# Gated mix of local and full attention on one core: the last rows of the first two tiles computed behind all others, first weights in larger pieces, and copies of the last units on VectorE

## The chip, the core and the metric

The kernel runs on one core of one Trainium2 chip. A core has five engines, each with an instruction queue of its own that is worked off in order: TensorE (PE: matrix products; PEld is its loading of weights), VectorE (DVE), ScalarE (ACT), GpSimd (POOL) and SyncE (SP, which here only issues transfers). They meet at semaphores. Transfers between main memory and the on-chip memory run on 16 DMA engines; in this kernel they are issued by SP, and a few of the first ones by ACT, and each of the two issuers has a queue of its own. Matrix products land in PSUM, eight banks of 128 rows by 512 numbers.

The metric is the time of one execution in microseconds (us) on the device. Before the change it was 901.09 us, the median of three runs from 900.93 to 901.24.

## The reference

Two attentions over the same 2048 rows of 448 numbers, 16 heads of 28 each, are mixed by a gate computed from the input. The setup draws all inputs in float32.

```python
x = A_x
g = _sigmoid((x * gate_w).sum(-1, keepdims=True))
a = _A_ref(x, A_wqkv, A_wo)    # each row attends to 8 earlier rows, 2 apart
b = _B_ref(x, B_wqkv, B_wo)    # each row attends to all rows
return g * a + (1 - g) * b

# _B_ref
q, k, v = qkv[0], qkv[1], qkv[2]
scores = jnp.einsum("bhqd,bhkd->bhqk", q, k) * (Dh ** -0.5)
p = _softmax(scores, axis=-1)
o = jnp.einsum("bhqk,bhkd->bhqd", p, v)
return (lambda x, *d: x.transpose(*d))(o, 0, 2, 1, 3).reshape(B, S, D) @ wo
```

## The kernel before

**Two parts of each number.** The products want more precision than one pass of the matrix engine gives. So a value is split into a rounded part (`hi`, type fp32r) and the rest (`lo` = value minus `hi`), and a product is the sum of hi by hi, hi by lo and lo by hi. The rounding is a copy (on ACT, `split` at L223, or a cast on DVE), the rest is a subtraction (on DVE or POOL).

**First stage: the projections.** The 448 input rows (the transposed input has one row for each of its 448 features) make three blocks of 128 and a tail of 64. The tail's `hi` stands in one half of the 128 partitions and its `lo` in the other, and the tail of the weights is loaded twice (`both`, L228), so that one product of the tail does the work of two. A tile of the result is 128 columns of weights by 512 input columns (a quarter `nb` of the 2048 positions), and takes 11 products (`ORDER`, L294): a triple (a, c, k) says whether the `lo` of the input (a) or of the weights (c) is used, and which block of rows (k). The first ten tiles (`FULL`) sum all their products in one PSUM bank (`project`, L314); after that tiles are cut in halves that run side by side. The list `tiles` (L449) fixes the order of the tiles; the first three use the three blocks of columns of weight set 0: columns 448 to 576 (place `wa`, 128 to 256, in `wh0`/`wl0`), 0 to 128, and 576 to 704. Tile 0 has an order of its own, `FIRST` (L296), and three products on zeros (`warm(3)`) behind its first one. Before it nine such products run while nothing has been loaded (`warm(9)`, L215). When a tile is done, `qk_tile` (L352) copies it out, splits it and stores both parts to main memory.

**The first loads** (L403 to L418). In the order of the program: the weights of tile 0 (`wr0`, three blocks of 128 columns, SP), blocks 0 and 1 of the first quarter of the input (ACT's queue), its block 2 and its tail (SP), the weights' tails for two tiles, the weights of tile 1 and then of tile 2 (`wr1`, 128 columns each), the third tail, and then the other three quarters of the input. A transfer from the ninth on is issued when the eighth before it has landed, since eight semaphores are used in turn. From L419 follow the roundings and rests: ACT first makes four zero tiles (`QP`, L422) that are wanted much later, then rounds the weights of tile 0, input block 2, the tail and the other weights; DVE rounds input blocks 0 and 1 and makes the rests; POOL makes the rest of tile 0's weights (L429). The splitting of the second quarter of the input (`split_x(1)`) stands behind tile 0, that of the third tile's weights (`split_third`) ahead of it.

**Second stage: full attention.** 16 units of 16 steps. Unit u has four heads (u // 4) and a quarter of the queries (u % 4); step kt has 128 of the keys. A step (`scores`, L966) makes 12 products for the scores of four heads into four PSUM banks, two exponentials of 128x1024 on ACT (L994) and, one step later, four products with V into the bank pair of `av` (L952, L955; each is shown as two rows). As long as maxima of later units are still to be found, a step also has up to three products of a first pass (L144) and the maxima of them on DVE (L150). The last maxima are done in step 234 of 256; the 21 steps from there have none, and I call them the **bare steps**. At a unit's end `fin_copy` takes `av` out of PSUM (it stands one step into the next unit, before that step's exponentials on ACT, and the next product into `av` waits for it); the sums are inverted, spread, multiplied (`fin_on`, POOL), and `fin_hi` rounds the result, `fin_lo` makes its rest and `fin_store` stores both. For unit 13 `fin_hi` comes in step 237, for unit 14 in step 255, `fin_copy` of unit 14 in step 241. `load_q` (L117) loads the next unit's queries in step kt = 12, together with its maxima (`nm`), which stand in two extra rows of the same tile.

The local attention's vector work runs on POOL and DVE beside this. In the last two units DVE also splits the weights of the output projection (`split_wo`, L782).

**Third stage: the output projection**, 16 tiles of 21 products (`op_tile`, L933; products at L841), whose first nine products are put ahead of the last products with V.

## Time and profile before

| | |
|---|---|
| median of the runs shown | 901.09 us (900.93 to 901.24) |
| the profiled execution's own time | 900.67 us |
| its span, first to last instruction | 898.9 us |
| busy: PE, DVE, ACT, POOL | 892.2, 738.2, 644.5, 641.0 us |
| first product on PE (on zeros) begins | 1.45 us |
| first product on data begins | 5.74 us |
| scores of the first bare step begin (see the second stage) | 782.55 us |
| last product of the output projection ends | 895.25 us |

The profiled execution was 0.42 us shorter than the median of the runs. Between its own time and its span lie 1.8 us that no engine shows.

How to read the rows: a timeline row gives start and duration in us, the engine, the source line, the operation, what it writes and reads with shapes, how many instructions were merged into the row, and in brackets how long the engine had been idle before it and what it waited for. An engine named with a q (SPq, ACTq) is the engine's queue issuing a transfer. A row of windows gives for each engine the busy us and the number of instructions in a stretch, then the clock that PE was granted (1.00 is full), the mean busy share of the DMA engines, and what they moved in GB/s. Matrix products overlap, so that a row's duration is longer than the distance at which such products follow each other.

### The profile page before, as it was taken

To read this page: it belongs to the slowest core of one execution; us is meant where nothing else is said; L and a number is where in the kernel's file an instruction comes from. 1 tells how busy PE (TensorE), PEld (TensorE's weight loads), DVE (VectorE), ACT (ScalarE), POOL (GpSimd) and SP (SyncE) were. 2 spreads that over 40 slices of the span, in tenths; PEclk is the share of its full clock that TensorE was granted. 3 is DMA by queue.
4 is the path that set the end of the run, shared out by engine and by line. 5 is a ranking of instruction groups with operands and counts; after the bars stand their busy time and mean duration, and the time that the engine had idled before them with its cause. 6 is when DMAs were issued, how large, how long until landed. Compare 5 with 4: busy or idle time off the path is not lost.

```text
span 898.9 us, 20542 instructions
## 1 busy us (share of the span) xinstructions
PE 892.2 (99%) x8326; PEld 533.8 (59%) x8326; DVE 738.2 (82%) x961; ACT 644.5 (72%) x770; POOL 641.0 (71%) x507
## 2 busy tenths in 40 slices
PE   8999999999999999999999999999999999999998
PEld 6888999999954444444444444444444444434997
DVE  6588999999979999999999999999999999821220
ACT  7456434343378888898988989889888898898220
POOL 2489846464469689999999999999999699501000
PEclk9999999999999999999999999999999999999999
DMA  8887403459472241225224242342220322245791
GB/s 267 282 252 191 151 12 84 134 139 104 120 243 70 94 132 46 76 50 157 70 57 145 82 116 67 84 137 65 56 65 19 89 43 57 75 104 156 220 285 53
DMA packets 116470, 104.51 MB, mean 116 GB/s; under 512 B 77160, under 2 KB 84712, under 8 KB 115592
## 3 DMA queue, kind: packets, MB, share of 16 engines
q1 hardware_dynamic: 116088, 102.68, 41.6%
q8 instruction: 65, 1.06, 0.5%
q10 hardware_dynamic: 288, 0.52, 0.2%
q14 instruction: 29, 0.24, 0.1%
HBM read 62.20 MB, written 40.96 MB: 115 GB/s over the span
## 4 chain that ended last, share of the span: by engine, by line
PE 98%; ACT 1%; DMA 1%; SPq 0%; issue 0%; DVE 0%; ACTq 0%
PE T L989 31%; PE av L955 28%; PE r L312 15%; PE T L841 8%; PE r L307 8%; PE r L144 4%; PE T L144 4%; DMA raw<-in_wB 1%; ACT P L994 0%; SPq L230 0%; ACT raw L375 0%; PE av L1039 0%; SPq L240 0%; ACT wh L224 0%; ACT onhi L892 0%
## 5 line engine op out<-in xcount | busy, mean ns | idle before, releaser
L994 ACT ACTIVATE P<-T 128x1024 f32<-128x1024 f32 x512 | 496.7, 1024 | 59.9 <-PE T L989 57.6
L150 DVE TENSOR_REDUCE MX<-T 128x1 f32<-128x512 f32 x470 | 442.1, 954 | 33.9 <-PE T L144 19.1
L955 PE MATMUL av<-P,V 128*32 128x512 f32 x2048 | 272.7, 605 | 0.4 <-ACT osb L859 0.4
L989 PEld LDWEIGHTS T<-QH,KH 30*128 30x128 f32 x1024 | 92.6, 181 | 230.6 <-ACT P L994 197.3
L144 PE MATMUL T<-KH,QP 28*128 28x512 f32 x704 | 220.0, 455 | 0.1
L989 PE MATMUL T<-QH,KH 30*128 30x512 f32 x1024 | 212.6, 489 | 0.2 <-ACT P L994 0.2
L166 DVE TENSOR_REDUCE MX<-r 128x2 f32<-128x1024 f32 x160 | 192.5, 1221 | 22.8 <-PE r L144 20.2
L989 PE MATMUL T<-QH,KL 28*128 28x512 f32 x1024 | 187.0, 395 | 0.0
L989 PE MATMUL T<-QL,KH 28*128 28x512 f32 x1024 | 184.9, 392 | 0.0
L618 POOL TENSOR_TENSOR prod<-qt,kt 128x896 f32<-128x896 f32 x64 | 135.4, 2115 | 5.1 <-DMA kt<-a_scr 5.0
L375 ACT ACTIVATE raw<-r 128x896 f32<-128x896 f32 (+1 forms) x64 | 58.9, 921 | 96.8 <-PE r L312 94.5
L144 PE MATMUL r<-KH,QP 64*128 64x512 f32 x320 | 105.0, 392 | 0.0
L679 POOL TENSOR_TENSOR oat<-oat,prod 128x896 f32<-128x896 f32 x48 | 101.3, 2110 | 2.0
L144 PEld LDWEIGHTS T<-KH,QP 28*128 28x128 f32 x704 | 86.0, 181 | 27.4 <-ACT P L994 19.4
L376 POOL TENSOR_TENSOR ast<-raw 128x448 f32<-128x448 f32 x48 | 55.5, 1155 | 57.9 <-ACT raw L375 48.2
L674 POOL TENSOR_TENSOR prod<-vt,L 128x896 f32<-128x896 f32 x56 | 95.4, 1704 | 0.2
L989 PEld LDWEIGHTS T<-QL,KH 28*128 28x128 f32 x1024 | 94.2, 184 | 0.0
L989 PEld LDWEIGHTS T<-QH,KL 28*128 28x128 f32 x1024 | 93.5, 183 | 0.5
L312 PE MATMUL r<-wh,xh 64*128 64x448 f32 (+1 forms) x512 | 93.3, 363 | 0.0
L955 PEld LDWEIGHTS av<-P,V 128*32 128x32 f32 x2048 | 40.3, 108 | 77.8 <-issue 65.0
L312 PEld LDWEIGHTS r<-wh,xh 64*128 64x128 f32 x512 | 75.1, 185 | 0.4
L312 PE MATMUL r<-wh,xl 64*128 64x448 f32 (+1 forms) x384 | 73.4, 364 | 0.0
(112 smaller groups left out, 1120.7 us busy)
## 6 DMA issues: line engine op xcount, KB each, us to landing
a_scr<-ast SPq DMA_DIRECT2D x24, 448.0 KB
qk_hi<-qkh SPq DMA_DIRECT2D x24, 256.0 KB
qk_lo<-qkh SPq DMA_DIRECT2D x24, 256.0 KB
rbc<-rs SPq DMA_DIRECT2D x64, 64.0 KB
QP<-qk_hi SPq DMA_DIRECT2D x64, 56.0 KB
KL<-qk_lo SPq DMA_DIRECT2D x16, 224.0 KB
QH<-qk_hi SPq DMA_DIRECT2D x64, 56.0 KB
QL<-qk_lo SPq DMA_DIRECT2D x64, 56.0 KB
```

Source lines behind the costliest of these rows:

```text
L144: nc.tensor.matmul(bank, qhis[u][h % 2][r, 128 * qs:128 * qs + 128], KH[u // NB % 3][r, 512 * kc:512 * kc + 512], start=True, stop=True)
L150: i = nc.vector.tensor_reduce(MX[:, n % NMX:n % NMX + k], bank, axis=X, op=ALU.max)
L166: nc.vector.tensor_reduce(m, PM[k], axis=X, op=ALU.max)
L307: nc.tensor.matmul(bank, ws[c][rows, k, t[4]:t[4] + 128], x, start=first, stop=last)
L312: nc.tensor.matmul(bank[:, 0:cols], x, ws[c][rows, k, 0:cols], start=first, stop=last)
L618: nc.gpsimd.tensor_tensor(out=p, in0=qt[c], in1=kvt["k", c % 2][:, HALO - DIL * w:HALO - DIL * w + NJ, :], op=ALU.mult)
L674: nc.gpsimd.tensor_tensor(out=dst.rearrange("p j (h d) -> p j h d", d=DH), in0=kvt["v", c % 2][:, HALO - DIL * w:HALO - DIL * w + NJ, :].r ...
L679: nc.gpsimd.tensor_tensor(out=ows[c % 2][:, :, 0:56] if w == W - 1 else oat[c], in0=oat[c], in1=oat[c, w], op=ALU.add)
L841: writes(bank, nc.tensor.matmul(bank[:, :D], src, wo[c][k], start=(first and k == ks[0] and i == 0), stop=(last and k == ks[-1] and i == 2)))
L955: nc.tensor.matmul(av[32 * h:32 * h + 32, :], V[:, kt, 4 * g + h, :], tiles_[h], start=(kt == 0), stop=(kt == NJ - 1), skip_group_check=True)
L989: nc.tensor.matmul(bank[a], (KH[g % 3], KH[g % 3], KL[g % 2])[t][r, ks], (qh, ql, qh)[t][r, :], start=(t == 0), stop=(t == 2))
L994: e = nc.scalar.activation(p, one if a == "2" else mine, AF.Exp, scale=SCALE).ins
```

## The change

Three groups of edits.

**The first loads.** The weights of tile 0 and of tile 2 (columns 448 to 704) are loaded in one transfer of 256 columns, the weights of tile 1 in a second one; all three blocks of the first quarter of the input go by ACT's queue; the weights' tails are loaded as 256 and 128 columns in place of 128, 128 and 128. Only two of the four zero tiles are made first.

**The first products.** Tiles 0 and 1 both get an order of their own, without the products of the tail rows (k = 3); these four follow behind both tiles. Tile 0 now has its first rest-of-input product in second place and mixes blocks as their parts are made; tile 1 does hi by hi, lo by hi, hi by lo. `warm(3)` is gone. ACT rounds input blocks 1 and 2 (before: 2 alone), DVE makes all rests of the weights, three blocks in one instruction (before: POOL for tile 0's, single blocks for the others). Both tiles are copied out behind tile 1, and the splitting of the second quarter stands behind them.

**The last units.** `fin_copy` of unit 14 and `fin_hi` of units 13 and 14 run on DVE; the queries of unit 15 are loaded three steps earlier than its maxima.

```diff
-    def load_q(u):
+    def load_q(u, low=True):
         Qs[u] = load_part(u, "QH", qk_hi), load_part(u, "QL", qk_lo)
+        if low:
+            load_nm(u)
+
+    def load_nm(u):
...
-        FIRST = [(0, 0, 0), (0, 1, 0), (0, 0, 1), (0, 1, 1), (0, 0, 2), (0, 1, 2),
-                 (1, 0, 0), (1, 0, 1), (1, 0, 2), (0, 0, 3), (0, 1, 3)]
+        FIRST = [[(0, 0, 0), (1, 0, 0), (0, 0, 1), (0, 1, 0), (0, 1, 1), (0, 0, 2), (0, 1, 2), (1, 0, 1), (1, 0, 2)],
+                 [(0, 0, 0), (0, 0, 1), (0, 0, 2), (1, 0, 0), (1, 0, 1), (1, 0, 2), (0, 1, 0), (0, 1, 1), (0, 1, 2)]]
...
         def project(n):
-            order = FIRST if n == 0 else ORDER
+            order = FIRST[n] if n < 2 else ORDER
             for i, p in enumerate(order):
-                product(n, p, None, i == 0, i == len(order) - 1)
-                if n == 0 and i == 0:
-                    warm(3)
+                product(n, p, None, i == 0, n > 1 and i == len(order) - 1)
+            if n == 1:
+                for m in range(2):
+                    product(m, (0, 0, 3), None, False, False)
+                    product(m, (0, 1, 3), None, False, True)
...
-        nc.sync.dma_start(wr0, wB[0:384, 448:576].rearrange("(k p) c -> p k c", p=128))
-        load_x(0, 0, 1, nc.scalar)
-        load_x(0, 1, 2, nc.scalar)
-        load_x(0, 2, 3)
+        nc.sync.dma_start(wr0[:, :, 0:256], wB[0:384, 448:704].rearrange("(k p) c -> p k c", p=128))
+        for kt in range(3):
+            load_x(0, kt, kt + 1, nc.scalar)
+        nc.sync.dma_start(wr1, wB[0:384, 0:128].rearrange("(k p) c -> p k c", p=128))
         load_tails(0, 1)
...
-        for t in (*QP[0], *QP[1]):
+        for t in QP[0]:
             nc.scalar.activation(t, t0, AF.Copy)
...
+        nc.vector.tensor_copy(xh[0][:, 0, :], r[:, 0, :])
+        low_x(0)
+        split(wh0[:, 0:3, wa], wl0[:, 0:3, wa], wr0[:, :, 0:128])
+        for kt in (1, 2):
+            nc.scalar.activation(xh[0][:, kt, :], r[:, kt, :], AF.Copy)
+            low_x(kt)
+        split(wh0[:, 0:3, wb], wl0[:, 0:3, wb], wr1)
+        nc.scalar.activation(tail[0:64], t[0:64], AF.Copy)
         nc.vector.tensor_tensor(out=tail[64:128], in0=t[0:64], in1=tail[0:64].bitcast(F32), op=ALU.subtract)
...
+        split(wh0[:, 3, 0:384], wl0[:, 3, 0:384], wt0[:, 0:384])
+        split(wh0[:, 0:3, wc], wl0[:, 0:3, wc], wr0[:, :, 128:256])
+        for t in QP[1]:
+            nc.scalar.activation(t, t0, AF.Copy)
...
-                qk_tile(n, t[2], t[3])
+                for m in {0: (), 1: (0, 1)}.get(n, (n,)):
+                    qk_tile(m, *tiles[m][2:4])
...
-            if n == 0:
+            if n == 1:
                 split_x(1)
...
-        nc.scalar.activation(t, av, AF.Copy)
+        if u == NU - 2:
+            nc.vector.tensor_copy(t, av)
+        else:
+            nc.scalar.activation(t, av, AF.Copy)
...
-        nc.scalar.activation(fin["hi"], fin["on"], AF.Copy)
+        if NU - 4 < u < NU - 1:
+            nc.vector.tensor_copy(fin["hi"], fin["on"])
+        else:
+            nc.scalar.activation(fin["hi"], fin["on"], AF.Copy)
...
-            if kt == 12 and u + 1 < NU:
+            if u + 2 < NU and kt == 12:
                 load_q(u + 1)
+            elif u + 2 == NU and kt == 9:
+                load_q(u + 1, False)
+            elif u + 2 == NU and kt == 12:
+                load_nm(u + 1)
```

How the instructions stand on the engines that the prediction speaks of. First, PE at the start of the program, before the change; `r_140` takes the products on zeros, `r_128` is the bank of tile 0 and `r_132` that of tile 1, `xh`/`xl` are the two parts of the input, `wh`/`wl` of the weights. Rows that read the same as one shown are left out here and below.

```order
L213 MATMUL r_140<-t_161 128x512 x9
L307 MATMUL r_128<-xh_180,wh_188 128x512
L213 MATMUL r_140<-t_161 128x512 x3
L307 MATMUL r_128<-xh_180,wl_189 128x512
L307 MATMUL r_128<-xh_180,wh_188 128x512
L307 MATMUL r_128<-xh_180,wl_189 128x512
L307 MATMUL r_128<-xh_180,wh_188 128x512
L307 MATMUL r_128<-xl_184,wh_188 128x512 x3
L307 MATMUL r_132<-xh_180,wh_188 128x512 x4
```

And the same place after it:

```order
L217 MATMUL r_140<-t_161 128x512 x9
L311 MATMUL r_128<-xh_180,wh_188 128x512
L311 MATMUL r_128<-xl_184,wh_188 128x512
L311 MATMUL r_128<-xl_184,wh_188 128x512 x2
L311 MATMUL r_132<-xh_180,wh_188 128x512 x3
L311 MATMUL r_132<-xl_184,wh_188 128x512 x3
L311 MATMUL r_132<-xh_180,wl_189 128x512 x3
L311 MATMUL r_128<-xh_180,wh_188 128x512
L311 MATMUL r_132<-xh_180,wl_189 128x512
L311 MATMUL r_136<-xh_180,wh_188 128x512 x4
```

Tile 0 now ends, but for its tail, with two products that need the rest of input blocks 1 and 2; tile 1's nine follow, then the four of the tails, and only then tile 2 (`r_136`).

Second, ACT at the start, after the change; `raw` is the wide piece of weights, `wr_192` the weights of tile 1, `wt_191` the tails.

```order
L423 ACTIVATE QP_155<-t_161 128x512
L423 ACTIVATE QP_156<-t_161 128x512
L228 ACTIVATE wh_188<-raw 128x3x128
L436 ACTIVATE xh_180<-V 128x512 x2
L228 ACTIVATE wh_188<-wr_192 128x3x128
L439 ACTIVATE xh_180<-V 64x512
L228 ACTIVATE wh_188<-wt_191 128x384
L228 ACTIVATE wh_188<-raw 128x3x128
L444 ACTIVATE QP_157<-t_161 128x512
L444 ACTIVATE QP_158<-t_161 128x512
L362 ACTIVATE qkh<-r_128 128x512
```

Input blocks 1 and 2 are now both rounded by ACT (the row with x2), between the weights of tile 0 and those of tile 1.

Third, DVE in the last units, after the change; `osb` is the copy of `av`, `onhi` the rounded result of a unit, and the rows on `wor` are the splitting of the output weights.

```order
L894 CAST onhi<-on 128x512
L683 STREAM_TRANSPOSE tw<-ow 128x256
L782 CAST KH_152<-wor 128x448
L783 TENSOR_TENSOR KL_153<-wor,KH_152 128x448
L858 COPY osb<-av 128x512
L782 CAST KH_3263<-wor 128x448
L783 TENSOR_TENSOR KL_153<-wor,KH_3263 128x448
```

The copy of `av` stands behind the fourth of the seven pieces of output weights and ahead of the fifth; before, the seven stood together.

More of the change, by code (lines that the diff above doesn't have):

```diff
@@ L400, in gated_mix_kernel @@
         wsets = {0: (wh0, wl0)}
-        wr0, wt0, wr1 = ptile("wr0"), ptile("wt0"), raw3()
-        wr0 = wr0[:, 0:384].rearrange("p (k c) -> p k c", k=3)
-        nc.sync.dma_start(wr0, wB[0:384, 448:576].rearrange("(k p) c -> p k c", p=128))
-        load_x(0, 0, 1, nc.scalar)
-        load_x(0, 1, 2, nc.scalar)
-        load_x(0, 2, 3)
-        load_tails(0, 1)
-        both(wt0[:, 0:256].rearrange("p (a c) -> p a c", a=2),
-             wB[384:448, 0:896].rearrange("p (a c) -> p a c", a=2)[:, :, 0:128])
-        nc.sync.dma_start(wr1[:, :, 0:128], wB[0:384, 0:128].rearrange("(k p) c -> p k c", p=128))
-        nc.sync.dma_start(wr1[:, :, 128:256], wB[0:384, 576:704].rearrange("(k p) c -> p k c", p=128))
-        both(wt0[:, 256:384], wB[384:448, 576:704])
+        wr0, wt0, wr1 = raw3(), ptile("wt0"), ptile("wr1")
+        wr1 = wr1[:, 0:384].rearrange("p (k c) -> p k c", k=3)
+        nc.sync.dma_start(wr0[:, :, 0:256], wB[0:384, 448:704].rearrange("(k p) c -> p k c", p=128))
+        for kt in range(3):
+            load_x(0, kt, kt + 1, nc.scalar)
+        nc.sync.dma_start(wr1, wB[0:384, 0:128].rearrange("(k p) c -> p k c", p=128))
+        load_tails(0, 1)
+        both(wt0[:, 128:384], wB[384:448, 448:704])
+        both(wt0[:, 0:128], wB[384:448, 0:128])
         load_tails(1, 2)
@@ L418, in gated_mix_kernel, with low_x @@
         load_x(3)
-        wa = slice(128, 256)
         nc.scalar.activation(zt, zt, AF.Exp)
-        for t in (*QP[0], *QP[1]):
+        for t in QP[0]:
             nc.scalar.activation(t, t0, AF.Copy)
-        nc.scalar.activation(wh0[:, 0:3, wa], wr0, AF.Copy)
         r, t = xst[:, 0, 0:3, :], xst[:, 0, 3, :]
-        nc.scalar.activation(xh[0][:, 2, :], r[:, 2, :], AF.Copy)
         tail = xh[0][:, 3, :]
-        nc.scalar.activation(tail[0:64], t[0:64], AF.Copy)
-        nc.scalar.activation(wh0[:, 3, 0:256], wt0[:, 0:256], AF.Copy)
-        nc.gpsimd.tensor_tensor(out=wl0[:, 0:3, wa], in0=wr0, in1=wh0[:, 0:3, wa].bitcast(F32), op=ALU.subtract)
-        for kt in range(3):
-            if kt < 2:
-                nc.vector.tensor_copy(xh[0][:, kt, :], r[:, kt, :])
+        wa, wb, wc = slice(128, 256), slice(0, 128), slice(256, 384)
+        def low_x(kt):
             nc.vector.tensor_tensor(out=xl[0][:, kt, :], in0=r[:, kt, :], in1=xh[0][:, kt, :].bitcast(F32),
                                     op=ALU.subtract)
-        nc.vector.tensor_tensor(out=tail[64:128], in0=t[0:64], in1=tail[0:64].bitcast(F32), op=ALU.subtract)
-        nc.vector.tensor_tensor(out=wl0[:, 3, 0:256], in0=wt0[:, 0:256], in1=wh0[:, 3, 0:256].bitcast(F32),
-                                op=ALU.subtract)
-        for kt in range(3):
-            split(wh0[:, kt, 0:128], wl0[:, kt, 0:128], wr1[:, kt, 0:128])
-        def split_third():
-            c = slice(256, 384)
-            for kt in range(3):
-                split(wh0[:, kt, c], wl0[:, kt, c], wr1[:, kt, 128:256])
-            split(wh0[:, 3, c], wl0[:, 3, c], wt0[:, c])
+        nc.vector.tensor_copy(xh[0][:, 0, :], r[:, 0, :])
[6 more added lines that the diff above has]
+        nc.scalar.activation(tail[0:64], t[0:64], AF.Copy)
+        nc.vector.tensor_tensor(out=tail[64:128], in0=t[0:64], in1=tail[0:64].bitcast(F32), op=ALU.subtract)
+        split(wh0[:, 3, 0:384], wl0[:, 3, 0:384], wt0[:, 0:384])
+        split(wh0[:, 0:3, wc], wl0[:, 0:3, wc], wr0[:, :, 128:256])
+        for t in QP[1]:
+            nc.scalar.activation(t, t0, AF.Copy)
         tiles = []
@@ L473, in gated_mix_kernel @@
                     split_w(w, range(i, i + k))
-            if n == 0:
-                split_third()
             if n in (3, 5):
@@ L487, in gated_mix_kernel @@
                 a_tile(n, t[2], t[3])
-            if n == 0:
+            if n == 1:
                 split_x(1)
```

## The prediction, made before the changed kernel ran

> **What bounds the kernel now.** I read the page first: busy shares and the chain of work that ended last.

> ```profile
> PE 892.2 (99%) x8326; PEld 533.8 (59%) x8326; DVE 738.2 (82%) x961; ACT 644.5 (72%) x770; POOL 641.0 (71%) x507
> PE 98%; ACT 1%; DMA 1%; SPq 0%; issue 0%; DVE 0%; ACTq 0%
> ```

> PE works 99% of the span and has 98% of the chain. What can be won is only PE time in which it waits, or work taken from it. So I looked for stretches where PE stands or is slowed, first at the start.

> ```profile
> 1.45:5.11 3.66, 3.66 (x9) 2.61 (x9) 0.58 (x1) 3.42 (x6) 3.35 (x2) 1.00 0.72 209
> 5.11:8.97 3.86, 3.24 (x13) 2.02 (x12) 3.44 (x5) 2.62 (x7) 0.96 (x1) 1.00 1.07 251
> 8.97:12.46 3.49, 3.26 (x15) 2.55 (x14) 3.21 (x11) 2.25 (x8) 0.00 (x0) 1.00 0.91 285
> 12.46:37.54 25.08, 25.08 (x129) 20.29 (x129) 14.07 (x21) 14.12 (x25) 4.60 (x5) 1.00 0.92 307
> ```

> The first window holds the nine products on zeros, which do no work. In the second PE is busy 3.24 of 3.86 us, in the third 3.26 of 3.49; from 12.46 on it never stands. The gap is in the two tiles up to 12.46, which the change rewrites. The timeline names the waits:

> ```profile
> 4.50 0.58 DVE L432 CAST xh<-V 128x512 fp32r<-128x512 f32 x1 [3.06 <-DMA V<-in_xT]
> 5.18 0.51 ACT L423 ACTIVATE wh<-wr 128x384 fp32r<-128x384 f32 x1
> 5.74 0.50 PE L307 MATMUL r<-xh,wh 128*128 128x512 f32 x1 [0.62 <-ACT wh L423]
> 6.07 0.86 PE L213 MATMUL r<-t 128*128 128x512 f32 x3
> 6.87 0.63 ACT L425 ACTIVATE xh<-V 128x512 fp32r<-128x512 f32 x1 [1.18 <-DMA V<-in_xT]
> 7.05 1.29 DVE L433 TENSOR_TENSOR xl<-V,xh 128x512 fp32r<-128x512 f32 x2
> 8.12 0.85 PE L307 MATMUL r<-xl,wh 128*128 128x512 f32 x3
> 9.20 0.47 PE L307 MATMUL r<-xh,wh 128*128 128x512 f32 x1 [0.23 <-ACT wh L224]
> 9.90 1.09 PE L307 MATMUL r<-xh,wh 128*128 128x512 f32 x4
> 12.46 1.09 PE L307 MATMUL r<-xh,wh 128*128 128x512 f32 x4
> 15.00 1.09 PE L307 MATMUL r<-xh,wh 128*128 128x512 f32 x4
> ```

> Tile 2 starts at 12.46 and tile 3 at 15.00: 11 products in 2.54 us, 0.231 us each. The 22 products of tiles 0 and 1 need 22 x 0.231 = 5.08 us, but take from 5.74 to 12.46, 6.72 us. So 1.64 us are lost there: to the three products on zeros at 6.07, to the wait for input block 2 (ACT starts on it at 6.87, the DMA having kept it 1.18 us), and to the tail's weights, which PE reaches at 8.12 + 0.85 = 8.97 and gets at 9.20.

> The second place is the 21 bare steps, from 782.55 us. The rows are the products with V, one row a step:

> ```profile
> 785.55 1.06 PE L955 MATMUL av<-P,V 128*32 128x512 f32 x8
> 787.89 1.06 PE L955 MATMUL av<-P,V 128*32 128x512 f32 x8
> 789.80 1.06 PE L955 MATMUL av<-P,V 128*32 128x512 f32 x8
> 793.80 1.06 PE L955 MATMUL av<-P,V 128*32 128x512 f32 x8
> 796.37 1.06 PE L955 MATMUL av<-P,V 128*32 128x512 f32 x8 [0.44 <-ACT osb L859]
> 798.27 1.06 PE L955 MATMUL av<-P,V 128*32 128x512 f32 x8
> ...
> 804.36 1.07 PE L955 MATMUL av<-P,V 128*32 128x512 f32 x8
> 806.26 1.06 PE L955 MATMUL av<-P,V 128*32 128x512 f32 x8
> 808.36 1.06 PE L955 MATMUL av<-P,V 128*32 128x512 f32 x8
> ```

> Undisturbed, steps follow at 1.90 and 2.10 us in turn (804.36, 806.26, 808.36), 4.00 for two. Two are longer: 785.55 to 787.89 is 2.34, and 793.80 to 796.37 is 2.57, where PE stood 0.44 us for `osb`. ACT's rows of that stretch say why:

> ```profile
> 785.38 0.63 ACT L892 ACTIVATE onhi<-on 128x512 fp32r<-128x512 f32 x1
> 785.90 3.81 ACT L994 ACTIVATE P<-T 128x1024 f32<-128x1024 f32 x4
> 795.71 0.60 ACT L859 ACTIVATE osb<-av 128x512 f32<-128x512 f32 x1
> 796.19 1.96 ACT L994 ACTIVATE P<-T 128x1024 f32<-128x1024 f32 x2
> ```

> The rounding of unit 13 (L892) and the copy of `av` (L859) stand between exponentials: 785.38 to 785.90 and 795.71 to 796.19, 0.52 and 0.48 us each in which no exponential begins.

> **The change, part by part.** *The end first, since its rows are there.* With the L892 at 785.38 gone, the pair of steps from 785.55 to 789.80 took 4.25 and takes 4.00: 0.25 won. With L859 gone, 793.80 to 798.27 took 4.47 and takes 4.00: 0.47. The first disturbance also swapped the order of long and short steps. If 2.10 and 1.90 simply go on from 785.55 (787.45, 789.55, 791.45, 793.55, 795.45), the product that waits for `osb` comes at 795.45 in place of 796.37: 0.92. Between 0.72 and 0.92 I take **0.80**.

> The third moved operation is worth nothing, and these rows show its cover:

> ```profile
> 824.18 0.63 ACT L892 ACTIVATE onhi<-on 128x512 fp32r<-128x512 f32 x1
> 824.70 1.94 ACT L994 ACTIVATE P<-T 128x1024 f32<-128x1024 f32 x2
> 827.37 1.07 PE L955 MATMUL av<-P,V 128*32 128x512 f32 x8
> 828.44 66.81 PE T L841 x327
> ```

> The exponentials behind L892 end at 824.70 + 1.94 = 826.64, while PE is busy with output products until 827.37. Cover 0.73 us. If PE comes to that place earlier, the exponentials come earlier too. From 828.44 the chain is one piece of 327 products to the end, so nothing else there moves but by shifting.

> What DVE pays:

> ```profile
> L850 DVE COPY res<-T x8: 392/624/626, 835.5 to 895.3; 128x448 f32<-128x448 f32 x7, 128x224 f32<-128x224 f32 x1
> 789.15 0.63 DVE L785 TENSOR_TENSOR KL<-wor,KH 128x448 fp32r<-128x448 f32 x1
> ```

> A copy of 448 columns out of PSUM took 0.62 us, so 512 take about 0.62 x 512 / 448 = 0.71, against 0.60 on ACT. But ACT could only begin at 795.71, behind two exponentials, though the last product into `av` ended at 793.80 + 1.06 = 794.86. DVE begins there if it is free: the copy stands behind the fourth piece of output weights, which ended at 789.15 + 0.63 = 789.78, 5 us earlier. It ends 0.71 us behind the product, when PE is still at the scores (their step takes 0.90 behind the same product). The cover is some 0.2 us; without it each 0.1 us of copy costs PE 0.1. Queued behind the copy are the last three pieces of output weights, wanted in the output projection 30 us later. On SP eight loads of queries now stand ahead of three of the output weights' loads and no longer behind the maxima's stores; the 5 us just named cover that. The roundings on DVE delay transposes and splits that nobody waits for.

> *The start.* PE's load is 22 products as before, three products on zeros fewer. What decides is when tile 0's last product (the rest of input block 2, by `wh`) can start, since from it on everything is in line: it, nine of tile 1 and four of the tails, 14 x 0.231 = 3.23 us to tile 2. Ahead of it: landing of block 2, its rounding on ACT 0.63 (the row at 6.87), its rest on DVE:

> ```profile
> L433 DVE TENSOR_TENSOR xl<-V,xh 128x512 fp32r<-128x512 f32 x3 | 2.0, 690 | 0.1
> L436 DVE TENSOR_TENSOR wl<-wt,wh 128x256 fp32r<-128x256 f32 x1 | 0.4, 426 | 0.0
> ```

> 0.69. So tile 2 starts at landing + 0.63 + 0.69 + 3.23 + about 0.10 of handing over = landing + 4.65. Before, block 2 landed at 6.87 at the latest. What changes is what flows beside it:

> ```profile
> 4.60:5.60 1.00, 0.52 (x3) 0.08 (x1) 0.97 (x2) 1.00 (x3) 0.20 (x1) 1.00 1.05 399
> 6.20:7.40 1.20, 1.20 (x6) 0.74 (x5) 1.17 (x2) 0.53 (x1) 0.53 (x1) 1.00 1.22 198
> ```

> Blocks 0 to 2 are 3 x 128 x 512 numbers, 0.79 MB, and the narrow first weights 0.20 MB. Now 0.39 MB of wide weights and 0.20 MB for tile 1 are queued beside the blocks, so up to 0.39 MB more can flow before block 2. At 399 GB/s (pieces of 2048 bytes, the first row) that is up to 1.0 us. On the other side, block 2 stands in ACT's queue with only blocks 0 and 1 ahead, so it can keep its 6.87. Bounds 6.87 and 7.85; I take 7.2, a third of the way, since the two queues share the engines and block 2 needs half the traffic of both at most. Tile 2 then starts at 11.85, **0.61 earlier**; the bounds give 0.94 earlier and 0.04 later.

> Do others bind? ACT has two zero tiles fewer ahead, so it is free before the 5.18 at which it rounded tile 0's weights (0.51). The wide ones land later, I assume near 5.5. Even if they land at 6.0, block 1 is rounded by 6.0 + 0.51 + 0.63 = 7.14, and block 2 is met on time. Tile 1's weights follow on ACT at 7.83 to 8.34, wanted at 8.85; their rest on DVE (384 columns, an estimate of 0.56 halfway between the rows of 256 and 512) ends near 9.1, wanted at 10.2; the tail's rest, the tail weights' rest and tile 2's rest end at 9.8, 10.4 and 10.9, wanted at 10.9, 11.2 and 12.8. The second quarter of the input is now rounded behind both tiles' copies: ACT has its third block near 14.8, PE wants it at 14.85 (the third product of tile 3). That is a cover of nothing, and a stall of 0.0 to 0.2; its load is issued sooner, because SP waits less. I count 0.

> POOL's 0.96 us for tile 0's rest (window 5.11:8.97) becomes 0.56 on DVE, ready earlier than before. `warm(3)` costs nothing to remove if PE keeps its clock. The rows show 1.00 throughout, with 3.86 - 3.24 = 0.62 us idle in the second window. After the change PE stands from 5.11 to about 5.5 + 0.51 = 6.0 before its first data, 0.9 us.

> [...]

> **Sum:** 0.80 + 0.61 = 1.4 us. The profiled execution's span goes from 898.9 to 897.5 and its time from 900.67 to 899.3; it lay 0.42 below the median, so against 901.09 I forecast **899.7**. This kernel's measurement tells about 0.2%, 1.8 us, from no change; 1.4 is inside.

> **Rivals.**

> *Block 2 lands no later than before, and the steps swap*: 0.94 + 0.92 = 1.86, and up to 0.2 more if block 2, alone in ACT's queue, lands sooner: 899.0 to 899.3. For it speaks that ACT's queue holds nothing else; against, that the wide weights share the engines from the first microsecond. 38%.

> *The start gives nothing*, because the wide weights and tile 1's all go ahead of block 2 (landing 7.85): only the end's 0.8 less 0.04, 900.3. 11%.

> *Slower: the first loads crawl.* If all 0.59 MB of weights go ahead of block 2 and at the 198 GB/s of the second row instead of 399, they take 3.0 instead of 1.5 us: block 2 lands at 7.85 + 1.5 = 9.35 and tile 2 starts at 14.0, 1.5 later; less the 0.8 of the end, the kernel is at 901.8. From a landing of 8.6 on (12.46 + 0.80 - 4.65), the end's gain is eaten. With PE idle for about 3 us, its clock could also fall to half, as products at twice 0.231 would show, which over such a wait's length costs about 1.5 more: 903.3. [...] Against it: at 4.60 to 5.60 both queues together moved 399 GB/s. 7%.

> *That DVE's copy is late* (the fourth piece of output weights ending after 794.9 instead of 789.78) would cost 1 us per us; it needs a load 5 us later, and I count it in the case before.

> **Numbers.** Forecast 44% (899.3 to 900.3), the faster rival 38%, nothing at the start 11%, slower 7%. Faster by over 0.2% (below 899.3): the faster rival, 38%. Slower by over 0.2% (above 902.9): the last with the fallen clock or a still later landing, 4%. The rest, 58%, within. The range holds eight in ten from the first three: 898.9 to 900.6.

> **What would show it.** The start of `r` for tile 2 (third bank) near 11.85; ACT's rounding of block 2 at 7.2; DVE's rest of 384 columns in about 0.56. Products with V of unit 15's first step near 795.4 less the start's gain, with no idle for `osb`, and steps of 1.90 and 2.10 throughout. I am wrong if block 2 lands after 7.85, if PE stalls in tile 3, if the clock falls below 1.00, or if PE waits for DVE's `osb`.

## The result, and the profile after

| | before | after |
|---|---|---|
| median of six runs each, us | 901.01 (900.70 to 901.53) | 904.64 (903.22 to 905.81) |
| profiled execution, us | 900.67 | 904.45 |
| its span, us | 898.9 | 902.7 |
| tile 2's first product, us | 12.46 | 16.48 |
| `av` product of the first bare steps (785.55 before) to that at 804.36 before, us | 18.81 | 17.95 |

The change made the kernel slower: ratio 1.0039, 95% interval 1.0026 to 1.0052. The forecast was 899.7 with a range up to 900.6.

The page of after, busy shares and the chain that ended last:

```profile
PE 894.2 (99%) x8323; PEld 526.9 (58%) x8323; DVE 738.7 (82%) x959; ACT 642.7 (71%) x763; POOL 639.7 (71%) x506
PE 96%; SPq 1%; DMA 1%; ACT 1%; DVE 0%; issue 0%; ACTq 0%; DVEq 0%
```

PE now does three products fewer and is busy 2.0 us longer. Longer busy with less work means slower products. The windows of the start show where (us, busy time and instructions of PE, PEld, DVE, ACT, POOL, then PE's granted clock, DMA share, GB/s; the clock column shows 1.00 also where the trace has no record of the clock yet, here ahead of 5.06 us):

```profile
1.45:5.44 3.99, 3.99 (x9) 2.82 (x9) 0.13 (x1) 2.54 (x4) 3.34 (x2) 1.00 0.74 186
5.44:11.07 5.63, 2.84 (x9) 1.62 (x9) 3.28 (x6) 2.86 (x6) 0.00 (x0) 0.77 0.96 293
11.07:15.55 4.48, 4.48 (x12) 3.49 (x11) 1.83 (x4) 1.72 (x4) 0.00 (x0) 0.53 0.76 235
15.55:16.48 0.93, 0.93 (x6) 0.75 (x5) 0.00 (x0) 0.27 (x1) 0.00 (x0) 1.00 1.07 174
16.48:41.56 25.08, 25.08 (x129) 20.14 (x129) 15.37 (x23) 14.84 (x27) 4.53 (x5) 1.00 0.88 289
```

Two things stand there: from 5.44 to 11.07 PE is idle for 2.79 us, and until shortly ahead of 15.55 it runs at about half its clock (recorded from 8.47 to 15.30). From 16.48 on, 129 products take 25.08 us, as they did before from 12.46 on. The timeline of after names the waits:

```profile
5.31 0.43 DVE L432 CAST xh<-V 128x512 fp32r<-128x512 f32 x1 [3.87 <-DMA V<-in_xT]
6.22 0.52 ACT L228 ACTIVATE wh<-raw 128x384 fp32r<-128x384 f32 x1 [1.52 <-DMA raw<-in_wB]
6.79 0.50 PE L311 MATMUL r<-xh,wh 128*128 128x512 f32 x1 [1.35 <-ACT wh L228]
9.36 0.63 ACT L436 ACTIVATE xh<-V 128x512 fp32r<-128x512 f32 x1 [1.66 <-DMA V<-in_xT]
10.05 0.79 PE L311 MATMUL r<-xh,wh 128*128 128x512 f32 x1 [1.21 <-ACT xh L436]
11.92 1.48 PE L311 MATMUL r<-xh,wh 128*128 128x512 f32 x3
13.20 1.48 PE L311 MATMUL r<-xl,wh 128*128 128x512 f32 x3
16.48 1.09 PE L311 MATMUL r<-xh,wh 128*128 128x512 f32 x4
```

Each engine that starts on fresh data was kept by a DMA: block 0 is taken at 5.31 (before 4.50), the weights at 6.22 (before 5.18), block 2 at 9.36 (before 6.87). And three products from 11.92 to 13.20 are 0.43 us apart, in place of 0.231: half clock. Tile 2 starts 4.02 later than before.

At the end the change does what it should:

```profile
790.12 1.06 PE L959 MATMUL av<-P,V 128*32 128x512 f32 x8
798.11 1.06 PE L959 MATMUL av<-P,V 128*32 128x512 f32 x8
808.07 1.07 PE L959 MATMUL av<-P,V 128*32 128x512 f32 x8
799.24 0.69 DVE L858 COPY osb<-av 128x512 f32<-128x512 f32 x1 [4.51 <-PE av L959]
```

The products at 790.12 and 808.07 are those that ran at 785.55 and 804.36: 17.95 us between them and not 18.81, so 0.86 won. DVE's copy begins 0.07 us behind the end of its product (798.11 + 1.06) and no product waits for it.

Elsewhere this profile loses little: 0.15 us by small drifts, and 0.42 near 598 us, where DVE waited for sums stored and loaded again:

```profile
598.07 0.25 DVE L873 RECIPROCAL finv<-fsum 128x16 f32<-128x16 f32 x1 [0.51 <-DMA fsum<-rs]
```

4.02 + 0.15 + 0.42 - 0.86 = 3.73; the spans differ by 3.8.

### The profile page after: what moved, and what is told of

Same layout as the page of the kernel before. It is cut to its first block, busy times and chain, and to the rows that moved or that the text cites. A ratio compares the mean times of both kernels' runs of the same rounds, so it can differ in the third digit from the quotient of the medians.

```text
span 902.7 us, 20523 instructions
## 1 busy us (share of the span) xinstructions
PE 894.2 (99%) x8323; PEld 526.9 (58%) x8323; DVE 738.7 (82%) x959; ACT 642.7 (71%) x763; POOL 639.7 (71%) x506
## 3 DMA queue, kind: packets, MB, share of 16 engines
q8 instruction: 65, 1.06, 0.5%
## 4 chain that ended last, share of the span: by engine, by line
PE 96%; SPq 1%; DMA 1%; ACT 1%; DVE 0%; issue 0%; ACTq 0%; DVEq 0%
PE T L993 30%; PE av L959 27%; PE r L316 15%; PE r L311 8%; PE T L839 8%; PE r L148 4%; PE T L148 4%; DMA V<-in_xT 1%; SPq L689 1%; SPq L99 0%; ACT P L998 0%; DVE MX L154 0%; DMA fsum<-rs 0%; ACT raw L381 0%; ACTq L240 0%
```

## The experiments

Theory: the end gains as forecast, and the start loses twice, by a late block 2 and by the clock that falls because PE then stands. The rivals are given with each run. Each ratio is against the kernel before on the same chip in the same session. Its median was 901.37 beside the end's edits (first run), the start's edits, the zeros in the waits and the transfers of before; 901.44 beside the two runs on parts of the transfers, the run without the zeros of before and tile 1's weights ahead; 901.58 beside the other four.

**The end's edits alone**, twice, put into the kernel before:

```diff
+        if u == NU - 2:
+            nc.vector.tensor_copy(t, av)
...
+        if NU - 4 < u < NU - 1:
+            nc.vector.tensor_copy(fin["hi"], fin["on"])
...
+            elif u + 2 == NU and kt == 9:
+                load_q(u + 1, False)
```

> Theory A (the loss is all at the start: input block 2 lands late and the clock falls; the end gains what was forecast): only the edits of the last units are in, so the time is 901.0 less about 0.85, 900.15, with tile 2 at 12.46 as before and no wait for the copy of av. Rival (the end gains only while PE comes late from a slow start): no gain, 900.9 to 901.1.

> The kernel before with the end's edits alone, a second time, beside the others on the same chip. Theory A (the end's edits gain 0.9 us whatever the start): 0.6 to 1.2 us under the kernel before. Theory B (what the earlier run showed was the spread between executions): within 0.3 us of it.

Measured 900.47 (ratio 0.999, 0.9981 to 0.9998) and 900.33 (0.9987, 0.9978 to 0.9996), 0.90 and 1.25 us less than the kernel before. In the second run the same two products stand at

```profile
785.82 1.06 PE L965 MATMUL av<-P,V 128*32 128x512 f32 x8
803.77 1.06 PE L965 MATMUL av<-P,V 128*32 128x512 f32 x8
```

17.95 us apart again. The end's 0.86 is shown, and this version beats the kernel before by about 0.1%.

**The start's edits alone** (the diff without the hunks just shown):

> Only the edits of the first loads and products. Theory A: 904.6 + 0.85 = 905.5, tile 2 about 4 us later than before, a stretch of granted clock 0.50. Rival (the two parts hang together): as the whole change, 904.6.

Measured 906.30 (1.0052, 1.0037 to 1.0068): tile 2 at 16.20, block 2 taken at 9.62. So the whole loss comes from the start. Here the clock did not fall: full clock is recorded first from 14.35, and until then products that followed each other were 0.43 us apart. The profile lost 1.36 us more near 211 us; that is taken up at the end of this section.

**Zeros in the waits**, in the whole change. The products of zeros do no work for the output; they only keep PE busy.

```diff
-    warm(9)
+    warm(12)
...
+                if n == 0:
+                    warm({1: 2, 4: 5}.get(i, 0))
```

> The whole change, with ten more products on zeros: three ahead of the first data, two behind tile 0's second product, five behind its fifth, where PE stood 1.35, 0.23 and 1.21 us. Theory A: the clock stays 1.00, block 2 still lands near 9.3, tile 2 starts near 14.0 instead of 16.48, time about 902.2. Rival (the half clock is not set by PE's idle time in a window): 0.50 stays in the rows, tile 2 at 16 or later, 904.6 or more. Rival (the late block alone costs all): tile 2 near 16.4.

Measured 902.50 (1.0010, 1.0000 to 1.0019). First its rows (timeline and windows), then the windows of after, both cut on the grid of the trace's records of the clock (a record stands where the clock changes; within a trace such times lie whole multiples of 3.41 us apart):

```profile
9.57 0.63 ACT L438 ACTIVATE xh<-V 128x512 fp32r<-128x512 f32 x1 [1.72 <-DMA V<-in_xT]
14.33 1.09 PE L311 MATMUL r<-xh,wh 128*128 128x512 f32 x4
...
4.46:7.87 3.41, 2.25 (x10) 1.47 (x9) 1.68 (x3) 1.40 (x3) 0.34 (x1) 1.00 1.06 334
7.87:11.28 3.41, 3.19 (x14) 2.25 (x13) 1.74 (x3) 1.71 (x4) 0.00 (x0) 1.00 0.87 256
```

```profile
5.06:8.47 3.41, 1.83 (x7) 0.79 (x5) 2.37 (x4) 1.15 (x2) 0.00 (x0) 1.00 1.04 313
8.47:11.88 3.41, 2.20 (x6) 1.49 (x5) 1.82 (x3) 2.52 (x6) 0.00 (x0) 0.50 0.85 278
11.88:15.29 3.41, 3.41 (x9) 2.64 (x8) 1.05 (x3) 0.91 (x2) 0.00 (x0) 0.50 0.73 229
```

With the zeros PE was busy 2.25 of 3.41 us and kept its clock; in after it was busy 1.83 and had 0.50 for the next two windows. Block 2 came as late as ever, and tile 2 started at 14.33. So of the 4.02 us, 16.48 - 14.33 = 2.15 are the clock's and 14.33 - 12.46 = 1.87 the landing's. These are two single profiles, and block 2 was taken 0.21 later in the one with the zeros, so the split is good to about 0.2.

**The transfers of before**, in the whole change:

```diff
-        nc.sync.dma_start(wr0[:, :, 0:256], wB[0:384, 448:704].rearrange("(k p) c -> p k c", p=128))
-        for kt in range(3):
-            load_x(0, kt, kt + 1, nc.scalar)
...
+        nc.sync.dma_start(wr0, wB[0:384, 448:576].rearrange("(k p) c -> p k c", p=128))
+        load_x(0, 0, 1, nc.scalar)
+        load_x(0, 1, 2, nc.scalar)
+        load_x(0, 2, 3)
...
```

> The whole change with the transfers of before (narrow weights, block 2 on SP's queue, order of before). Theory A: block 2 lands near 6.9, the weights of tile 1 near 8.6 and bind, tile 2 near 12.15, clock 1.00, time about 899.9. Rival (the new order of products and the rests on DVE cost the time themselves): tile 2 at 13.5 or later, above 901.

Measured 901.83 (1.0006, 0.9997 to 1.0015). Its start:

```profile
8.68 0.52 ACT L228 ACTIVATE wh<-raw 128x384 fp32r<-128x384 f32 x1 [1.14 <-DMA raw<-in_wB]
9.25 0.96 PE L311 MATMUL r<-xh,wh 128*128 128x512 f32 x3 [0.44 <-ACT wh L228]
12.36 1.09 PE L311 MATMUL r<-xh,wh 128*128 128x512 f32 x4
```

The loss of the start is gone, so the late landing came from the transfers and not from the new order of products. But next to nothing is won, and Theory A's 12.15 and 899.9 are missed: now tile 1's weights come last. That the time is still over the kernel before has other places (below).

**Which part of the transfers**, two runs: block 2 moved back to SP's queue in the whole change, and block 2 alone put third on ACT's queue with the transfers of before.

```diff
-        for kt in range(3):
-            load_x(0, kt, kt + 1, nc.scalar)
+        load_x(0, 0, 1, nc.scalar)
+        load_x(0, 1, 2, nc.scalar)
+        load_x(0, 2, 3)
```

> The whole change, but input block 2 goes behind the first weights on SP's queue, ahead of tile 1's weights, instead of third on ACT's queue. Theory A (two causes that add: the wide first weights make everything behind them about 0.9 us later, as input block 0 landed at 5.29 instead of 4.48 and block 1 at 7.05 instead of 6.13, and the third place on ACT's queue puts 1.6 us more on block 2): block 2 lands near 7.7 instead of 9.34, tile 1's weights later than 7.87, tile 2 starts at 12.4 to 13.0, with the clock full or half as the window falls; about 901.3 us with a full clock, 903 with a fallen one. Theory B (the wide weights alone take the transfers' time, whatever the queue): block 2 lands at 9.0 or later and the time stays within 0.4 us of the change's.

> The change with the transfers of before (as in the earlier run where block 2 landed near 6.84 and tile 2 started at 12.36), and of the new transfers only one thing: block 2 third on ACT's queue. Theory A (the third place on the queue costs 1.6 us by itself): block 2 lands at 8.0 to 8.6, tile 2 starts at 12.7 to 13.4 with a full clock. Theory B (the wide weights alone make block 2 late): block 2 lands at 6.9 to 7.2 and nothing else moves, tile 2 at 12.2 to 12.5.

Measured 902.95 (1.0018, 1.0009 to 1.0027) and 901.84 (1.0000, 0.9991 to 1.0009). The rows of the first, then of the second:

```profile
8.06 0.63 ACT L437 ACTIVATE xh<-V 128x512 fp32r<-128x512 f32 x1 [0.22 <-DMA V<-in_xT]
14.36 1.09 PE L311 MATMUL r<-xh,wh 128*128 128x512 f32 x4
...
5.58:8.99 3.41, 1.90 (x7) 1.02 (x7) 2.14 (x4) 1.84 (x4) 0.00 (x0) 1.00 0.97 270
8.99:12.40 3.41, 3.41 (x9) 2.62 (x9) 2.70 (x5) 3.00 (x6) 0.00 (x0) 0.50 0.87 265
```

```profile
8.09 0.63 ACT L440 ACTIVATE xh<-V 128x512 fp32r<-128x512 f32 x1 [0.86 <-DMA V<-in_xT]
13.79 1.09 PE L311 MATMUL r<-xh,wh 128*128 128x512 f32 x4
```

When ACT takes block 2, right behind its landing:

| | block 2 second on SP | block 2 third on ACT |
|---|---|---|
| narrow first weights | 6.87 (before) | 8.09 |
| wide first weights | 8.06 | 9.36 (after) |

The wide piece costs 1.19 or 1.27 us, the place on the queue 1.22 or 1.30. The two add, to within the 0.2 us by which single profiles of the same transfers differ (9.36 and 9.49 in the change's two runs, 6.87 and 7.04 with the transfers of before), and Theory A stands, with about 1.2 us for each cause in place of its 0.9 and 1.6. In the right-hand column the wide weights come together with tile 1's weights, which there go ahead of the input's tail; the 1.27 is the price of both. Third on ACT's queue, block 2 stood behind two blocks; second on SP's, behind the first weights alone. How the two queues share the DMA engines no run here shows. In both runs tile 2 came later than landing plus 4.65, since the clock was half for a while: in the first a window with PE busy 1.90 was followed by one at 0.50; in the second full clock is recorded first from 10.94. So both missed the start that Theory A gave for tile 2 with a full clock.

**Block 2 on SP and zeros in the waits together:**

> The whole change with block 2 on SP's queue behind the first weights, and with the zero products in the waits (12 ahead, 2 behind tile 0's second product, 5 behind its fifth) that kept the clock full in an earlier run, where block 2 landed at 9.57 and tile 2 started at 14.33. Left out is nothing; products of zeros are added whose result is not read. Theory A (landing and clock are two causes that add): block 2 lands at 8.0 as in the run without zeros, the clock stays full, tile 2 starts at 12.7 to 13.0, and the time is 901.0 to 901.8 us. Theory B (the landing does not matter as long as the clock is full): tile 2 at 14 or later, 902.5 us.

Measured 902.30 (1.0009, 1.0000 to 1.0018). The chain of waits of this run, in order of time (start, duration, what):

```profile
7.49 0.64 ACT xh L439
8.13 0.04 issue
8.17 0.97 PE r L311 x3
9.14 1.16 PE r L217 x5
10.29 7.91 PE r L311 x34
```

The clock stayed full (6.81 to 7.04 us, and from 8.51 on, products followed each other at 0.23), and block 2 was rounded right behind block 1, but tile 2 started at 14.06 and not by 13.0. The five zeros (L217) now stand on the chain for 1.16 us, ahead of products whose data is there. By its figures this is Theory B's outcome, but the block did come early and the zeros took the gain. Without the five, by an estimate from the chain, tile 2 would start at 14.06 - 1.16 = 12.9. Zeros that fill a wait become a cost once the wait is gone.

**The zeros of the kernel before taken away**, and nothing else:

```diff
-                if n == 0 and i == 0:
-                    warm(3)
```

> The kernel before without the three products of zeros behind its first product, and nothing else. Left out is only work whose result is not read. Theory A (a clock window of 3.41 us in which TensorE is busy for less than about 2.1 us halves the clock for what follows): TensorE is busy for about 2.0 of the window's 3.41 us instead of 2.79, so the clock falls in some executions or in all, depending on where the windows lie, and the time is 1 to 2.5 us longer in those. Theory B (my prediction's reading, that only an idle window does it): the clock stays full, and the time within 0.3 us of the kernel before.

Measured 901.52 (1.0000, 0.9991 to 1.0009). The profiled execution was the longest of ten, 902.68, and in it full clock is recorded only from 10.74:

```profile
7.36 0.63 PE L307 MATMUL r<-xh,wh 128*128 128x512 f32 x1
7.79 0.63 PE L307 MATMUL r<-xh,wl 128*128 128x512 f32 x1
10.77 0.40 PE L307 MATMUL r<-xh,wl 128*128 128x512 f32 x1
13.55 1.09 PE L307 MATMUL r<-xh,wh 128*128 128x512 f32 x4
```

Products 0.43 apart until about 10.7 put tile 2 at 13.55, 1.09 late. The other nine took 900.87 to 901.85. That the missing zeros did this is not shown: with its zeros, the kernel before had two executions of 33 at 902.80 and 902.86 in the same session. Nor is it the fall that Theory A expected: the clock had not risen yet, and PE was busy 3.10 us, not about 2.0, in the window from 3.91 to 7.32. In the median the zeros are worth nothing that can be measured, as Theory B has it.

**Can the new order gain with other transfers?** Both are the whole change with the transfers of before and one or two moves more. First tile 1's weights moved ahead of the tails, behind block 2; then, in addition, the last piece of the tails' weights ahead of tile 2's (the lines show the new places; the old ones are left out):

```diff
         load_x(0, 2, 3)
+        nc.sync.dma_start(wr1[:, :, 0:128], wB[0:384, 0:128].rearrange("(k p) c -> p k c", p=128))
         load_tails(0, 1)
...
+        both(wt0[:, 256:384], wB[384:448, 576:704])
         nc.sync.dma_start(wr1[:, :, 128:256], wB[0:384, 576:704].rearrange("(k p) c -> p k c", p=128))
```

> The change with the transfers of before, in which tile 1's weights now go ahead of the tails on SP's queue, right behind block 2. Where the transfers of before stood, tile 1's weights were the last to land for the first nine products and TensorE waited 0.44 us there. Theory A (what the new order of products is worth is set by the later of block 2 and tile 1's weights): tile 1's weights land at 7.3 to 7.9 instead of near 8.4, tile 2 starts at 11.5 to 12.0, 0.5 to 0.9 before the kernel before, and with the end's 0.9 the whole is 899.5 to 900.2 us. Theory B (the tails, which now land later, bind the last rows' products behind tile 1): tile 2 at 12.2 or later.

> As the run with tile 1's weights ahead, and the last rows' weights of columns 256 to 383 ahead of tile 2's weights on SP's queue. There the weights of the last rows landed at 9.98, since one conversion takes all their columns, and the second tail product waited for it until 11.23, so that tile 2 started at 12.03. Theory A (the last transfer that the first eleven products of each tile need sets tile 2's start): tile 2 starts at 11.5 to 11.8; with the end's gain of 0.9 the time is 899.4 to 900.2 us, 0.2 to 0.25 per cent under the kernel before. Theory B (tile 2's own weights, now later, bind instead): tile 2 starts at 12.0 or later, and the time is as that run's, near 901.5 on such a chip.

Measured 901.53 (1.0000, 0.9991 to 1.0009) and 901.72 (0.9998, 0.9989 to 1.0007). In the first, tile 2 started at 12.03, behind the tails' weights: tile 1's weights were early, as Theory A has it, but the tails bound, as Theory B has it, and the 899.5 to 900.2 us of Theory A are missed. The second, timeline:

```profile
6.87 0.63 ACT L440 ACTIVATE xh<-V 128x512 fp32r<-128x512 f32 x1 [0.19 <-DMA V<-in_xT]
11.62 1.09 PE L311 MATMUL r<-xh,wh 128*128 128x512 f32 x4
13.47 1.67 ACT L228 ACTIVATE xh<-V 128x512 fp32r<-128x512 f32 x3 [0.51 <-DMA V<-in_xT]
14.15 0.19 PEld L311 LDWEIGHTS r<-xh,wh 128*128 128x128 f32 x1 [0.26 <-ACT xh L228]
14.67 0.19 PEld L311 LDWEIGHTS r<-xh,wh 128*128 128x128 f32 x1 [0.33 <-ACT xh L228]
15.19 0.30 PEld L311 LDWEIGHTS r<-xh,wh 128*128 128x128 f32 x2 [0.34 <-ACT xh L228]
14.16 1.76 PE L311 MATMUL r<-xh,wh 128*128 128x512 f32 x4
15.76 1.09 PE L311 MATMUL r<-xh,wl 128*128 128x512 f32 x4
```

Tile 2 starts at 11.62, 0.84 before the old time, as Theory A has it; the time it gave is not reached. Tile 3 gives it back: its first four products take 15.76 - 14.16 = 1.60 us and not 4 x 0.231 = 0.92, three of them waiting for a block of the second quarter that ACT rounds, and ACT itself waited for the transfer. What is left is 0.16. The wait at the start has only moved one tile on.

**The change a second time:**

> The change, a second time, beside the others on the same chip. Theory A (a half-busy clock window follows from its transfers, wherever the windows lie): clock halved for one or two windows again, tile 2 starts at 15 or later, and the time 2.5 to 4.5 us over the kernel before. Theory B (the first run fell on unlucky windows): clock full in this profile, tile 2 near 14.3, and the time 1 to 1.5 us over.

Measured 905.01 (1.0034, 1.0022 to 1.0047), block 2 taken at 9.49, tile 2 at 16.07, products at half clock up to about 14. The loss is no accident of one session. The clock took another way to it, though: here it did not fall, but was not raised before 14.24.

**Open.** In the profiles of three runs with the new order of products and early transfers (the last two designs and the transfers of before) the bare steps come 2.0 to 3.1 us later, against the profiled execution of before, than their starts account for. Part of this lies in which execution was profiled: that of before, 900.67, was 0.7 to 0.9 under its medians in these sessions, and two of the three profiles, 902.98 and 902.65, were 1.15 and 0.93 over theirs. With the medians, the profiles' starts and the end's 0.86, an estimate of what is lost is 1.2 to 1.4 us, enough to eat the end's gain. Two places show it in their profiles. One is the wait for the stored sums (near 598 us after, 596 in the run below), 0.5 to 1.1 us lost. It does not hang on the new order: with the order of before, the first run of the end's edits and the run without the zeros lost 0.3 and 0.4 there, and the profiled execution of before nothing. The other is near 211 us; in the run with the transfers of before, DVE's rows there are

```profile
207.90 1.22 DVE L170 TENSOR_REDUCE MX<-r 128x2 f32<-128x1024 f32 x1 [0.27 <-PE r L148]
213.99 4.62 DVE L170 TENSOR_REDUCE MX<-r 128x2 f32<-128x1024 f32 x4 [2.30 <-PE r L316]
```

1.62 us were lost there, 1.31 and 1.70 in the last two designs, 0.80 in the change's second run, and none in its first (by the time from DVE's row that ends one unit's maxima to the next such row, 209.20 to 254.94 before). With the order of before it was 0.3 and 0.0 in the two runs of the end's edits and 0.0 without the zeros. The profile shows the scores that DVE waited for as done before. What held it is not settled, and no run was made for it.

## Why the prediction was wrong, step by step

The windows from the first product to the taking of block 2, before and after (the columns as above):

```profile
1.45:6.87 5.42, 4.80 (x14) 3.37 (x14) 1.99 (x3) 4.00 (x8) 4.32 (x3) 1.00 0.85 235
1.45:9.36 7.91, 5.81 (x14) 3.60 (x14) 2.37 (x4) 3.69 (x6) 3.34 (x2) 0.94 0.86 232
```

- **The landing of block 2**, put at 7.2 between 6.87 and 7.85: wrong, it was taken at 9.36. This is the step that failed, and the term of 0.61 that hangs on it became a loss. The upper bound let at most 0.39 MB more flow ahead of the block, at 399 GB/s, the rate of one microsecond of the trace before. By the rates of the two rows above, 5.42 x 235 = 1.27 MB and 7.91 x 232 = 1.84 MB were moved, an estimate: 0.56 MB more, at a mean rate that had not changed, which makes 2.4 of the 2.49 us. The argument that block 2, with only blocks 0 and 1 ahead of it in ACT's queue, "can keep its 6.87" was the wrong way round: the place behind two blocks costs 1.22 to 1.30 by itself. The slower rival had the direction right, but that its 9.35 is so near is luck: it adds 198 GB/s for the weights to the same bound of 7.85, and knows nothing of the place on the queue.
- **Tile 2 = landing + 4.65**: right where the clock is full and nothing else binds, 0.1 short. 9.57 gave 14.33, 6.87 gave 11.62.
- **"`warm(3)` costs nothing to remove if PE keeps its clock"**: the condition failed. PE's idle time was put at 0.9 us; in after it is 2.79, and 2.15 us went to the half clock. "The rows show 1.00 throughout" was misread for the start: the trace before has no record of the clock ahead of 4.35, and its first six products on zeros, from 1.45 to 4.18, were 0.46 us apart, twice the 0.231 of full clock. The slower rival had the fall of the clock at 1.5 us, too small. No run shows that 1.5, which was the author's estimate; what the runs showed in its place is the 2.15 us above, and a clock of 0.50 behind windows in which PE was still busy 1.83 (after) and 1.90 of 3.41 us (block 2 on SP).
- **Tile 3, counted 0 of 0.0 to 0.2**: 0.68 in the run where tile 2 came early. By an estimate from that run, whose transfers are others, the start would have gained about 0.2 and not 0.61 even with block 2 at 7.2.
- **The end, 0.80**: right, 0.86 and 0.86. DVE's copy took 0.69 (0.71 forecast); nobody waited for it.
- **The faster rival** (block 2 lands no later): fell with the first step, although it was given 38%.

## What to carry to other kernels

Here a first transfer was late by the wider piece loaded with it (1.19 and 1.27 us) and by a place further back on its queue (1.22 and 1.30), and the two added: count all that both queues can move ahead of the piece that binds, and price it at the mean rate that the trace shows up to that landing (235 GB/s here), not at the best microsecond (399). Before taking filler work off a waiting TensorE, sum its busy time, with the new waits in it, over stretches of 3.41 us, the step of the clock's changes in these traces: 1.83 and 1.90 us were too little here, 2.25 kept the clock. And when a tile is moved forward, look at what the tile behind it needs; here its input was no earlier, and the gain stopped there.

## What the runs showed of the hardware

What raises the clock is not settled. Every rise in the profiles cut on this grid came behind a window with PE busy 2.90 (before) to 3.41 us (after); but windows at half clock with 3.01 us (block 2 on ACT with the transfers of before) and 3.10 us (without the zeros of before) raised nothing, nor did those from 1.94 to 2.82 (both in the run of the start's edits alone).

Where this grid lies differed between executions: in the two profiles of the change, full clock is recorded first from 5.06 us (and lost again at 8.47) and first from 14.24, and 9.18 us is no multiple of 3.41. Whether this makes one and the same start slower in some executions, no run here shows.

The transfers up to the landing of block 2 ran at 235 GB/s before and 232 after; with the narrow weights and block 2 on ACT it was 219, an estimate from that run's windows (97, 292 and 227 GB/s from 0.70, 4.11 and 7.52 us on), and with block 2 on SP the two windows from 2.17 to 8.99 show 241 and 270. A single microsecond before reached 399. From before to after, what changed the landing was mostly how much went ahead of it.
